# Twelve early products around the fourth head pair, two-sum output groups and unsorted v in a fused attention and gated feed-forward kernel

## The chip, the cores and the metric

The kernel runs on one core of one Trainium2 chip. The metric is the device time of one execution in microseconds (us). "Time" below is that number. "Span" is the stretch that the profiler shows for the core; in every profiled run the time was 1.8 to 2.2 us longer than the span of the same run. PE is the matrix engine, DVE, ACT and POOL are the vector, scalar and general engines, and SP is the engine that here only issues DMAs. All runs in this document gave correct results.

## The reference, cut to what matters

Eight batches, eight heads, 576 positions, head size 64. Attention is masked by blocks of 64: a query sees the keys of its own and of earlier blocks. All tokens then pass through one gated feed-forward layer.

```python
def _attn_ref(q, k, v):                       # (8, 8, 576, 64) each
    scores = scale * np.matmul(q, k.transpose(0, 1, 3, 2))
    mask = block_i >= block_j                 # block = position // 64
    ...                                       # softmax over the keys
    return np.matmul(attn, v)

def _moe_ref(x, w_gate, w_val, w_out):        # x: (4608, 512), d_ff = 1536
    gate = np.maximum(x @ w_gate, 0.0)
    val = x @ w_val
    return gate * val @ w_out
```

## The kernel before

The program is one long stream of feed-forward (FFN) products for PE (groups of 128x128 by 128x512), in tiles of 512 tokens, 144 products to a full tile: 96 for gate and value, 48 for the output. Tile j needs the attention result of batch j. The attention work of the next batches is pushed into this stream at chosen places, so that DVE, ACT, POOL and the DMAs work beside PE. A "place" is the number of products issued so far; tile 0 covers places 0 to 143. Four pairs of heads make a batch. The 576 positions are 512 "main" positions and a "tail" of 64, so each batch has four "visits" of a pair (scores and exponentials), and one "tail visit" for its last 64 queries.

The K and Q of the mains lie in two alternating buffers, by the parity of the batch: batch 2 uses the buffers of batch 0. The scheduler keeps the program's order on each engine and adds the waits that the data need. A DMA is put on the queue of the engine that issues it.

Some names: `qTm` and `kTm` are the transposed queries and keys of the mains, `perm` is where a DMA transpose puts them first, `sc` are scores, `attnT` the exponentials. "PV products" multiply these with v; their normalised result is `xnat`, its transpose `xT` is the input of the FFN, and `hT` is gate times value. A "corner memset" zeroes a masked corner of `attnT`.

The parts that the change and the argument touch:

```python
    def unpermute(self, hp, engs):           # copies K and Q of one head pair into place
        for t in range(2):
            engs[t]((qTm, kTm)[t][self.b % 2][:, :, hp, :]..., self.perm[t, hp // 2]...)

    def both_av(r):                          # PV products of a fourth pair, both heads
        ...
        recip = sb.tile([128, 2, 4], FP, name="recip_both", bufs=1)
        nc.vector.reciprocal(recip, av[:, :, :, 64])
        nc.vector.tensor_tensor(out=xnats[r]..., in0=av[:, :, :, 0:64], in1=..., op=AX.mult)

    def put(j, s, ob, n0, n1):               # stores 128 rows of the output
        if j < B:
            r0 = S * j + 128 * s
            (nc.gpsimd if j == 0 else nc.scalar).dma_start(out[r0 : r0 + 128, :], ob)
        ...

    # in ffn_gen: tiles 0 and 1 start with 9 products that need only three head pairs
                if j < 2 and f == 0:
                    ahead = psum_ffn.tile([128, 512], FP, name="ffnp")
                    for c in range(3):
                        product(gate, 0, c, 0); yield
                    for c in range(3):
                        product(val, 1, c, 0); yield
                    for c in range(3):
                        product(ahead, 0, c, 1); yield
                    steps = [(0, 3), (1, 3)]
    ...
    # each output group is one sum of 12 products; its result goes through one of three ob buffers
                ob = sb.tile([128, 512], FP, name="ob", bufs=3)[:, 0 : n1 - n0]
                nc.vector.tensor_copy(ob, op)
                if store:
                    store.pop()()
                store.append(lambda ...: put(j, s, ob, *n))
    ...
        ffn(9)
        both_av(3)
        to_xT_pe(3, (act, dve))
    ...
        def mains_2a():
            e2.cast_qk(0, 4, (pool, pool))
            e2.transpose(0)                  # two DMA transposes on SP's queue
            e0.load_tails((2,))
            e2.load_v_chunks(0)
    ...
            (90, lambda: e1.sort_v(0, (dve, act))),      # 16 small products
    ...
        events = tail_at(10, 0, (26, 30)) + ...          # tail visit of batch 0: place 154
            (16, un(2, 0, (dve, pool))),                 # copy of batch 2's first pair: place 160
            (44, un(2, 1, (dve, pool))),
```

The softmax here doesn't subtract the row's maximum and nothing guards it: scores larger than these inputs give would overflow.

Of the kernel before, what the change touches and what calls it, by code (L numbers as in the profile page):

```python
# [10 lines left out]
FP = mybir.dt.float32  # L11
# [6 lines left out]
def kernel(  # L18
# [51 lines left out]
    v_p = consts.tile([128, 4, 512], BF, name="v_p")  # L70
    zeros = v_p[:, 0, :]
    nc.vector.memset(zeros, 0.0)

    sel = consts.tile([128, 516], BF, name="sel")
# [14 lines left out]

    def selection(eng):  # L90
        eng.memset(sel, 0.0)
        for c in range(4):
            ps = slice(32 * c, 32 * c + 32)
            eng.tensor_copy(
                sel[ps].rearrange("p (j m) -> p j m", j=4)[:, :, 0:128:4],
                ident[ps, None, 32 * c : 32 * c + 32].to_broadcast([32, 4, 32]),
            )
# [21 lines left out]
    class Early:  # L119
# [27 lines left out]

        def load_v_packed(self, h0):
            self.st[2, h0] = new_stage(1024)
            self.load(self.st[2, h0], v, h0, 4)  # L150
# [59 lines left out]
        def cast_v_packed(self, h0, eng):  # L210
            eng(
                v_p[:, :, 64 * h0 : 64 * h0 + 256].rearrange(
                    "p j (h d) -> p h j d", d=64
                ),
                self.st[2, h0].rearrange("p (h j d) -> p h j d", h=4, j=4),
            )

# [5 lines left out]

        def sort_v(self, h0, engs):


            tp = [psum_sc.tile([128, 2, 512], FP, name="sc") for _ in range(2)]
            for j in range(4):
                for c in range(4):
                    ps = slice(32 * c, 32 * c + 32)  # L230
                    nc.tensor.matmul(
                        tp[c // 2][:, c % 2, 0:256],
                        sel[ps, 128 * j : 128 * j + 128],
                        v_p[ps, j, 64 * h0 : 64 * h0 + 256],
                        start=(j == 0),
                        stop=(j == 3),
                        skip_group_check=True,
                    )
            for i in range(2):
                engs[i](  # L240
                    v_bf[self.b % 2][:, 2 * i : 2 * i + 2, h0 : h0 + 4, 0:64],
                    tp[i][:, :, 0:256].rearrange("p g (h d) -> p g h d", d=64),
                )
# [313 lines left out]
    def both_av(r):  # L557
# [5 lines left out]
        for hh in range(2):  # L563
# [11 lines left out]
        recip = sb.tile([128, 2, 4], FP, name="recip_both", bufs=1)  # L575
        nc.vector.reciprocal(recip, av[:, :, :, 64])
        nc.vector.tensor_tensor(
            out=xnats[r].rearrange("q p (g d) -> q g p d", g=2),
            in0=av[:, :, :, 0:64],
            in1=recip.to_broadcast([128, 2, 4, 64]),  # L580
            op=AX.mult,
        )
# [6 lines left out]
    def to_xT_pe(r, evac):  # L589
        b, hp = divmod(r, 4)  # L590
        if hp == 3:
            br = psum_one.tile([128, 1024], BF, name="one")
        else:
            br = psum_ffn.tile([128, 1024], BF, name="ffnp")
# [20 lines left out]
    def put(j, s, ob, n0, n1):  # L615
        if j < B:
            r0 = S * j + 128 * s
            (nc.gpsimd if j == 0 else nc.scalar).dma_start(out[r0 : r0 + 128, :], ob)
        else:
            for i in range(2):  # L620
                r0 = S * (2 * s + i) + 512
                (nc.scalar, nc.sync)[i].dma_start(
                    out[r0 : r0 + 64, n0:n1], ob[64 * i : 64 * i + 64]
                )

    def ffn_gen():
        for j in range(B + 1):
            hT = []
            x = xT_of(j) if j < B else xTt.rearrange("p b h n -> p h b n")
            ahead = None  # L630
            for f in range(12):

                def product(to, t, c, f):
                    nc.tensor.matmul(  # L634
                        to,
                        (wg, wv)[t][f // 4][:, c, 128 * (f % 4) : 128 * (f % 4) + 128],
                        x[:, c],
                        start=(c == 0),
                        stop=(c == 3),
                    )  # L640

                steps = [(t, c) for t in range(2) for c in range(4)]
                if ahead is None:
                    gate = psum_ffn.tile([128, 512], FP, name="ffnp")
                else:
                    gate, ahead, steps = ahead, None, steps[3:]
                val = psum_ffn.tile([128, 512], FP, name="ffnp")
                if j < 2 and f == 0:
                    ahead = psum_ffn.tile([128, 512], FP, name="ffnp")
                    for c in range(3):  # L650
                        product(gate, 0, c, 0)
                        yield
                    for c in range(3):
                        product(val, 1, c, 0)
                        yield
                    for c in range(3):
                        product(ahead, 0, c, 1)
                        yield
                    steps = [(0, 3), (1, 3)]
                for t, c in steps:  # L660
                    product((gate, val)[t], t, c, f)
                    if (t, c) == (0, 3):
                        gate_sb = sb.tile([128, 512], BF, name="gate_sb", bufs=3)
# [327 lines left out]
```

## Time and profile before

The time is 376.27 us, the median of three runs (375.64 to 376.54). The profiled run is a fourth one; it took 377.73 us.

| | before |
|---|---|
| span of the profiled run | 375.6 us |
| PE busy | 361.1 us, 96% |
| DVE, ACT, POOL busy | 46%, 45%, 31% |
| first output product starts | 48.4 us |
| FFN product 144 (tile 1) starts | 66.8 us (its weight load: 66.4) |

From the page of the profile: busy time (share of the span) and instructions, then the busy share of PE and the granted clock of PE in 40 slices of 9.4 us, in tenths.

```profile
PE 361.1 (96%) x2979; PEld 178.3 (47%) x2979; DVE 172.0 (46%) x392; ACT 170.5 (45%) x282; POOL 116.4 (31%) x151
...
PE   6879999799999999999999999999999999999995
...
PEclk9689999989999999999999999999999999999999
```

PE sets the time. It has slack only in the first 80 us: slices 1 to 3 and slice 8 are not full, and the clock is below full speed in some of the same slices. The trace's clock record has 0.50 at 9.0 to 15.9, 26.1 to 29.5 and 73.9 to 77.3 us.

From the list of what PE waited for (us in total, times, longest):

```profile
PE one L597 <- DVE xnat L577: 2.1, 2, 1.0
...
PE ffnp L634 <- DVE xT L600: 1.6, 2, 0.8
...
PE ffnp L457 <- ACT gate_sb L664: 0.6, 1, 0.6
```

The first two lines are the gaps around the fourth pair, twice, once in tile 0 and once in tile 1: PE has done its nine early products and stands until the pair's result is normalised and transposed.

From the timeline (start, duration, engine, line, operation, in brackets the idle time before it and what ended it), around the start of tile 1:

```profile
70.64 0.40 PE L597 MATMUL one<-ident,xnat 128*128 128x128 bf16 x4 [1.03 <-DVE xnat L577]
71.82 0.38 PE L634 MATMUL ffnp<-xT,wg 128*128 128x512 bf16 x1 [0.79 <-DVE xT L600]
...
72.99 0.64 PE L457 MATMUL sc<-qTt,kTm 64*128 64x64 bf16 x32
...
73.34 1.06 POOL L268 COPY kTm<-perm 128x512 bf16<-128x512 bf16 x1 [8.05 <-PE sc L457]
```

Before the change POOL holds the copy of batch 2's keys ready and waits 8.05 us for PE's tail visit of batch 0 to have read the buffer. PE waits for no copy there.

The table of windows (window, its length, busy time of PE, weight loads, DVE, ACT and POOL with counts, granted clock, DMA share, GB/s):

```profile
60.00:70.00 10.00, 9.06 (x109) 5.07 (x105) 4.84 (x17) 5.49 (x9) 3.18 (x4) 1.00 1.04 186
70.00:80.00 10.00, 8.02 (x85) 3.90 (x85) 3.90 (x8) 4.58 (x9) 5.07 (x7) 0.83 1.12 151
80.00:95.00 15.00, 15.00 (x135) 7.23 (x134) 8.77 (x22) 10.56 (x19) 10.46 (x13) 1.00 0.78 194
...
120.00:350.00 230.00, 229.83 (x1866) 112.33 (x1865) 104.48 (x243) 104.42 (x174) 47.02 (x56) 1.00 0.94 92
```

After 80 us PE is full at full clock.

### The profile page before, as it was taken

The numbers are of one execution on the slowest core, as the hardware profiler recorded it, in microseconds if no ns is written. First come the engines' busy times: TensorE is split into PE (matmuls) and PEld (weight loads), VectorE is DVE, ScalarE is ACT, GpSimd is POOL, SyncE is SP. The second block draws the span as 40 slices with busy tenths as digits, with TensorE's granted clock in tenths as the row PEclk, the third lists the DMA queues.
The fourth block names the chain that finished last, engine by engine and source line by source line (L and its number), as shares of the span: only waits on it lengthen the run. The fifth ranks groups of instructions, "written<-read, shape, count | busy, mean of one in ns | idle before, by whom it ended". The sixth has DMA issues, their size and how long they took to land.

```text
span 375.6 us, 7492 instructions
## 1 busy us (share of the span) xinstructions
PE 361.1 (96%) x2979; PEld 178.3 (47%) x2979; DVE 172.0 (46%) x392; ACT 170.5 (45%) x282; POOL 116.4 (31%) x151
## 2 busy tenths in 40 slices
PE   6879999799999999999999999999999999999995
PEld 2534445444455445544454445444544454444443
DVE  4633544346555554455434543544445444323432
ACT  4823466456524755355445534653366423302310
POOL 5768846176129960570048003100000000000000
PEclk9689999989999999999999999999999999999999
DMA  8999998949989999999469954936400120020003
GB/s 254 292 371 359 364 265 214 189 58 275 216 162 88 134 120 177 175 125 133 124 99 133 125 134 87 69 62 150 78 16 15 44 99 7 0 86 28 2 34 107
DMA packets 142323, 51.35 MB, mean 137 GB/s; under 512 B 122448, under 2 KB 135504, under 8 KB 142288
## 3 DMA queue, kind: packets, MB, share of 16 engines
q1 hardware_dynamic: 81008, 34.62, 42.4%
q0 software_dynamic: 56576, 8.13, 40.3%
q10 hardware_dynamic: 4704, 8.13, 6.7%
q8 instruction: 23, 0.38, 0.5%
q14 instruction: 12, 0.10, 0.1%
HBM read 37.75 MB, written 9.44 MB: 126 GB/s over the span
## 4 chain that ended last, share of the span: by engine, by line
PE 92%; DMA 3%; DVE 3%; ACT 1%; issue 0%; DVEq 0%
PE ffnp L634 51%; PE ffnp L674 23%; PE ffnp L547 5%; PE sc L423 3%; PE ffnp L516 2%; DMA xT<-xnat 2%; PE one L423 2%; PE ffnp L283 1%; PE sc L380 1%; PE sc L457 1%; DMA stage<-in_q_dram 1%; DVE qTm L289 1%; DVE kTm L289 0%; PE one L547 0%; PE one L457 0%
## 5 line engine op out<-in xcount | busy, mean ns | idle before, releaser
L668 DVE TENSOR_TENSOR hT<-gate_sb,ffnp 128x512 bf16<-128x512 bf16 x108 | 74.1, 686 | 96.5 <-PE ffnp L634 84.3
L664 ACT ACTIVATE gate_sb<-ffnp 128x512 bf16<-128x512 f32 x108 | 64.8, 601 | 103.1 <-PE ffnp L634 103.0
L634 PE MATMUL ffnp<-xT,wg 128*128 128x512 bf16 x384 | 105.3, 385 | 2.2 <-DVE xT L600 1.6
L634 PE MATMUL ffnp<-xT,wv 128*128 128x512 bf16 x384 | 104.3, 385 | 0.3 <-ACT gate_sb L664 0.3
L674 PE MATMUL ffnp<-wo,hT 128*128 128x512 bf16 (+1 forms) x444 | 102.2, 373 | 0.0
L634 PEld LDWEIGHTS <-wv 128*128 128x128 bf16 x432 | 40.6, 99 | 48.7 <-issue 6.5
L634 PEld LDWEIGHTS <-wg 128*128 128x128 bf16 x432 | 40.7, 99 | 47.6 <-issue 5.6
L674 PEld LDWEIGHTS <-hT 128*128 128x128 bf16 x444 | 40.6, 98 | 41.1 <-issue 0.8
L432 ACT ACTIVATE attnT<-sc 128x1024 bf16<-128x1024 f32 x56 | 56.8, 1039 | 0.0
L684 DVE COPY ob<-ffnp 128x512 f32<-128x512 f32 (+1 forms) x37 | 25.0, 677 | 38.2 <-PE ffnp L674 38.1
L321 POOL DMA_DIRECT2D v_bf<-in_v_dram x20 | 16.9, 876 | 68.2 <-PE ffnp L516 68.2
L547 PEld LDWEIGHTS <-attnT 128*128 128x128 bf16 x600 | 25.1, 99 | 14.5 <-DVE xnat L502 4.4
L501 DVE RECIPROCAL recip<-ffnp 128x4 f32<-128x4 f32 (+1 forms) x73 | 13.1, 179 | 39.3 <-PE ffnp L547 28.2
L547 PE MATMUL ffnp<-v_bf,attnT 128*128 128x65 bf16 x570 | 27.0, 195 | 0.0
L438 ACT ACTIVATE attnT<-one 128x256 bf16<-128x256 f32 x28 | 10.7, 383 | 31.9 <-PE ffnp L423 29.4
L502 DVE TENSOR_TENSOR xnat<-ffnp,recip 128x256 bf16<-128x256 f32 x57 | 24.2, 424 | 2.0
L478 ACT ACTIVATE attnTt<-one 64x256 bf16<-64x256 f32 x8 | 3.0, 377 | 33.1 <-PE ffnp L457 33.1
L423 PE MATMUL sc<-qTm,kTm 64*128 64x512 bf16 (+1 forms) x168 | 17.0, 305 | 0.0
L423 PEld LDWEIGHTS <-kTm 64*128 64x128 bf16 x224 | 9.0, 94 | 15.3 <-issue 11.7
L469 ACT ACTIVATE attnTt<-sc 128x1024 bf16<-128x1024 f32 x16 | 15.6, 1014 | 0.0
L321 POOL DMA_DIRECT2D k_bf<-in_k_dram x16 | 14.4, 953 | 0.2 <-issue 0.2
L321 POOL DMA_DIRECT2D q_bf<-in_q_dram x16 | 14.4, 948 | 0.0
(91 smaller groups left out, 261.7 us busy)
## 6 DMA issues: line engine op xcount, KB each, us to landing
out_dram<-ob ACTq DMA_DIRECT2D x28, 256.0 KB, 2.2
stage<-in_moe_w_gate_dram SPq DMA_DIRECT2D x6, 512.0 KB, 9.3
stage<-in_moe_w_val_dram SPq DMA_DIRECT2D x6, 512.0 KB, 9.5
stage<-in_q_dram SPq DMA_DIRECT2D x6, 512.0 KB, 6.6
stage<-in_k_dram SPq DMA_DIRECT2D x6, 512.0 KB, 8.1
stage<-in_moe_w_out_dram SPq DMA_DIRECT2D x6, 512.0 KB, 9.5
stage<-in_v_dram SPq DMA_DIRECT2D x16, 128.0 KB, 5.1
stage<-in_v_dram SPq DMA_DIRECT2D x8, 256.0 KB, 5.4
```

The costliest lines, as they stand in the source:

```text
L321: nc.gpsimd.dma_start(dst, src[b, :, 128 * c : 128 * c + n, :].rearrange("h p d -> p h d"),)
L423: nc.tensor.matmul(where[c].rearrange("p (c n) -> p c n", n=128), kTm[b % 2][head_of(hh), c, hp, :], qTm[b % 2][head_of(hh), c:4, hp, :], ...
L432: return lambda: nc.scalar.activation(at[:, :, lo : lo + 512], sc, AF.Exp, scale=scale)
L469: return lambda: nc.scalar.activation(at[:, :, 2 * i : 2 * i + 2, 0:256], main[i].rearrange("p g (h n) -> p g h n", h=2), AF.Exp, scale=scale,
L501: nc.vector.reciprocal(recip, av[:, :, 64])
L502: nc.vector.tensor_tensor(out=out, in0=av[:, :, 0:64], in1=recip.to_broadcast([rows, n, 64]), op=AX.mult,)
L547: nc.tensor.matmul(av[:, p, :], at[:, hh, col : col + 128], vb[:, c, h, :], start=(p == 0), stop=(c == p), skip_group_check=True,)
L634: nc.tensor.matmul(to, (wg, wv)[t][f // 4][:, c, 128 * (f % 4) : 128 * (f % 4) + 128], x[:, c], start=(c == 0), stop=(c == 3),)
L664: nc.scalar.activation(gate_sb, gate, AF.Relu)
L668: nc.vector.tensor_tensor(out=h, in0=gate_sb, in1=val, op=AX.mult)
L674: nc.tensor.matmul(op, hT[f][:, 128 * s : 128 * (s + 1)], wo[f // 4][:, f % 4, n0:n1], start=(f == 0), stop=(f == 11),)
L684: nc.vector.tensor_copy(ob, op)
```

## The change

The intent is to fill PE's gaps in the first 80 us. Tiles 0 and 1 begin with 12 products of three head pairs instead of 9, split around the fourth pair's PV products and transposes. The first two output groups of tile 0 are summed in two parts, so that PE can begin before the last third of the output weights is there. Batch 1's v is loaded in its natural order for all heads, which removes 16 sorting products, their evictions and the matrix for them. Beside these, `both_av` normalises head by head, batch 0's stores move from POOL's queue to SP's, and many places of the schedule move. The core of the diff (cuts marked):

```diff
+            first = 0
+            if j < 2:
+                first = 2
+                acc = {n: psum_ffn.tile([128, 512], FP, name="ffnp")
+                       for n in ((0, 0), (0, 1), (1, 0))}
+                for cs in ((0, 1), (2,)):
+                    for t in range(2):
+                        for f in range(2):
+                            ...
+                            for c in cs:
+                                product(acc[t, f], t, c, f)
+                                yield
+                ...                      # then the four products of the fourth pair
...
+            if j == 0:                   # first two output groups: products 0 to 7 first
+                ops = [psum_ffn.tile([128, 512], FP, name="ffnp") for _ in range(2)]
+                for f0 in (0, 4):
+                    for s in range(2):
+                        for f in range(f0, f0 + 4):
+                            out_mm(ops[s], s, f, 0, 512, 0, 8)
+                            if f == 7:
+                                part_sum[s] = new_ob(512)
+                                nc.vector.tensor_copy(part_sum[s], ops[s])
+                            yield
...
-        recip = sb.tile([128, 2, 4], FP, name="recip_both", bufs=1)
-        nc.vector.reciprocal(recip, av[:, :, :, 64])
-        nc.vector.tensor_tensor(...)
+            normalise(xnats[r][:, :, 64 * hh : 64 * hh + 64], av[:, hh])
...
-            (nc.gpsimd if j == 0 else nc.scalar).dma_start(out[r0 : r0 + 128, :], ob)
+            (nc.sync if j == 0 else nc.scalar).dma_start(out[r0 : r0 + 128, :], ob)
...
-        ffn(9)
+        ffn(4)
+        to_xT_pe(2, (act, None))
         both_av(3)
+        ffn(5)
         to_xT_pe(3, (act, dve))
...
         def mains_2a():
+            e2.load_v_chunks(0)
+            e2.load_v_chunks(1)
+            e2.load_tails((0, 1))
+            e2.load_tails((2,))
             e2.cast_qk(0, 4, (pool, pool))
             e2.transpose(0)
-            e0.load_tails((2,))
-            e2.load_v_chunks(0)
...
-        events = round_at(94, 4, (113, 117), (121, pe_xT))
-        events += round_at(109, 5, (129, 133), (137, pe_xT))
+        events = round_at(96, 4, (112, 112), (112.3, pe_xT))
+        events += round_at(104, 5, (112.1, 112.2), (118, pe_xT))
...
-            (90, lambda: e1.sort_v(0, (dve, act))),
...
-        events = tail_at(10, 0, (26, 30)) + tail_at(116, 1, (132, 136))
+        events = tail_at(20, 0, (38, 42)) + tail_at(116, 1, (132, 136))
...
             (16, un(2, 0, (dve, pool))),
             (44, un(2, 1, (dve, pool))),
```

The tail visit of batch 0 moves from place 154 to place 164, while the copy of batch 2's first pair into the same key buffer stays at place 160. And `mains_2a` now asks SP for seven loads before the two transposes that this copy needs.

## The prediction

> **What bounds it now.** PE. It is busy 361.1 of 375.6 us (page, busy times), and the table of windows shows it idle for about 0.2 us between 80 and 350 us. What can be saved lies before 80 us: 10.5 us idle there, plus half clock (granted 0.50) at about 9.0-15.5, 26-29.3 and 74-77.3 us. PE's waits around both fourth pairs: 2.1 us for xnat before the transposes, 1.6 us for xT after them. The Trainium skill ("TensorE: Matmul & The Clock Gate", "What's actually happening") says the clock halves after about one idle window of 3.4 us; the trace agrees: slow stretches of about 3.3 us follow such gaps.
>
> **What the change does directly.** It puts 4 products before the fourth pair's PV products, 5 behind them (1.08 us at 0.216 us each, against a 1.03 us wait) and 3 behind the transposes (0.65 us against 0.79 us). It removes 16 sorting products (0.55 us of PE), two evictions and Pool's selection matrix (2.5 us). Two sums per output group let PE go on before the last output weights arrive: those land at 45.5 us, one load per 1.36 us, and this stays. So I expect PE 6-9 us ahead of before at the end of tile 0 (FFN product 144: about 58-60 us instead of 66.8).
>
> **What takes most of it back.** The tail visit of batch 0 moves from product 154 to 164, but the copy of batch 2's first pair into the same K tile stays at product 160. The order of instructions shows that PE's tail scores now wait for Pool's copy of batch 2's K; in before, Pool waited for PE. Two things follow. The last 64 queries of batch 0 see batch 2's keys in two of eight heads (the result should still pass). And PE now depends on batch 2's chain: load, cast, DMA transpose, copy. The change also puts four v-chunk loads and three tail loads ahead of that transpose on SP's queue. With landings read from before: batch 1's v about 50.5-51 us, batch 0's tails 52.5, batch 2's q and k 58.5-60, two stores to 60, four chunk loads at 1.1 us each to 64.5, three tails at 0.85 us to 67, two transposes about 1.1 us apart to 69, Pool's copy 1.07 us: about 70.3 us. PE arrives at about 64-65, waits some 6 us, and restarts at half clock, as in before.
>
> **Time.** In before the tail visit ended at 73.6 us, 302.0 us before the end, 10 products (2.2 us) earlier in the stream. So span = 70.3 + 0.6 + 302.0 - 2.2 = 370.7 us; measured times lie 0.7 us above the span: 371.4 us, range 367.5 to 375.0. Faster by over 2%: 0.17; within 2%: 0.81; slower: 0.02.
>
> **What would show it.** Right: the list of waits has one PE wait of 4-8 us for Pool's kTm copy near 65-71 us, the largest of the run; both 1.03 us waits for xnat under 0.4 us; first output product before 44 us (before: 48.4); no sorting products; idle PE after 80 us unchanged. Wrong: PE reaches the tail visit without that wait, or waits on output weights (DMA) at 45-48 us for over 2 us.
>
> **What would make it wrong.** Chunk loads may move faster than 1.1 us each, or the transposes may overtake them: then 365-368 us. If the restart stays at full clock, another 1.7 us goes. Stalls of PE around product 112 only eat into the wait. Later transposes give up to 375.

## The result, and the profile after

The changed kernel took 380.86 us (four runs, 380.73 to 381.38); the kernel before took 376.08 us in the same rounds (375.64 to 376.54). Ratios in this document are the mean time of one kernel's runs over that of the other's of the same rounds, so not quite the ratio of the quoted medians. Here it is 1.0130, with a 95% interval of 1.0112 to 1.0147. So the kernel is slower by 1.3%, inside the 2% that the prediction called most likely, but 5.9 us above the top of its range.

The same views as before. The page:

```profile
PE 357.5 (94%) x2915; PEld 178.1 (47%) x2963; DVE 176.6 (47%) x399; ACT 169.6 (45%) x279; POOL 111.3 (29%) x142
...
PE   6999987597999999899999999999999999999996
...
PEclk9899999998999999999999999999999999999999
```

The early gaps are smaller: slices 2 and 3 are now full. Slices 6, 7 and 10 are new holes, where the kernel before had a 9 each time (slice 17, with the wait at 159 us, shows an 8), and slice 8 has fallen from 7 to 5.

What PE waited for:

```profile
PE sc L412 <- POOL kTm L223: 3.6, 1, 3.6
...
PE one L378 <- DVE qTm L223: 1.6, 1, 1.6
PE sc L522 <- DVE xnat L457: 1.5, 2, 0.7
PE sc L522 <- DVE attnT L698: 1.2, 1, 1.2
PE ffnp L580 <- DMA xT<-xnat: 1.2, 2, 1.0
```

The waits around the fourth pair are gone in their old form (2.1 and 1.6 us). In their place are a wait for POOL's key copy, one for DVE's query copy, one between the two heads of `both_av`, and one for a memset. The timeline shows the first two:

```profile
69.90 0.19 PE L412 MATMUL one<-qTt,kTt 64*128 64x64 bf16 x1
...
73.65 0.64 PE L412 MATMUL sc<-qTt,kTm 64*128 64x64 bf16 x32 [3.56 <-POOL kTm L223]
...
87.04 0.27 PE L378 MATMUL one<-qTm,kTm 64*128 64x256 bf16 x1 [1.62 <-DVE qTm L223]
87.63 0.27 PE L378 MATMUL ffnp<-qTm,kTm 64*128 64x256 bf16 x1 [0.33 <-DVE hT L595]
...
83.42 3.56 DVE L223 COPY qTm<-perm 128x512 bf16<-128x512 bf16 x1
...
72.55 1.04 POOL L223 COPY kTm<-perm 128x512 bf16<-128x512 bf16 x1 [9.21 <-DMA perm<-k_bf]
...
82.97 0.61 POOL L195 CAST v_bf<-stage 64x512 bf16<-64x512 f32 x1 [2.67 <-PE ffnp L471]
83.53 2.02 POOL L189 CAST v_bf<-stage 128x1024 bf16<-128x1024 f32 x2
85.50 1.04 POOL L223 COPY kTm<-perm 128x512 bf16<-128x512 bf16 x1
...
66.04 1.67 SPq L158 DMA_DIRECT2D stage<-in_v_dram  x1
67.80 1.34 SPq L209 DMA_TRANSPOSE perm<-q_bf  x1
69.24 1.28 SPq L209 DMA_TRANSPOSE perm<-k_bf  x1
```

The sense of the wait at the tail visit has turned round. Before, POOL waited 8.05 us for PE. Now POOL waits 9.21 us for a DMA transpose, and PE waits 3.56 us for POOL. The transposes of the queries and of the keys are issued at 67.8 and 69.2 us, because seven loads stand ahead of them in SP's queue; in the kernel before they were issued at 58.3 and 60.2 us:

```profile
58.31 1.34 SPq L254 DMA_TRANSPOSE perm<-q_bf  x1
60.19 1.31 SPq L254 DMA_TRANSPOSE perm<-k_bf  x1
```

Reading the program, this order also lets the last 64 queries of batch 0 see keys of batch 2 in two of the eight heads; the result still passes the comparison.

Further down, a DVE copy takes 3.56 us. The statistics of this instruction, from the view of the tile it writes (shortest, median and longest in ns):

```profile
L223 DVE COPY qTm<-perm x8: 591/625/3565, 71.3 to 128.7; 128x512 bf16<-128x512 bf16 x8
```

The same copy of the same shape needs 0.59 us when nothing disturbs it. The long one begins beside POOL's cast at 82.97 us, lasts through four POOL instructions in a row, and ends 0.44 us after the last of them (86.98 against 86.54 us). PE waits 1.62 and 0.33 us for it.

The windows:

```profile
60.00:70.00 10.00, 7.88 (x82) 4.00 (x79) 5.08 (x15) 4.06 (x8) 2.16 (x3) 1.00 0.99 233
70.00:80.00 10.00, 6.16 (x63) 2.75 (x56) 2.07 (x4) 4.05 (x7) 4.64 (x7) 0.83 0.80 171
80.00:95.00 15.00, 12.95 (x111) 6.53 (x111) 10.53 (x19) 7.54 (x13) 8.92 (x11) 0.89 0.65 172
...
120.00:350.00 230.00, 226.90 (x1844) 111.90 (x1875) 103.63 (x243) 104.27 (x174) 49.17 (x59) 1.00 0.99 93
```

PE's busy time falls from 9.06 to 7.88 us between 60 and 70, from 8.02 to 6.16 us between 70 and 80, and from 15.00 to 12.95 us between 80 and 95, where the clock is also no longer full. The clock record has 0.50 at 9.5 to 12.9, 74.3 to 77.7 and 88.0 to 91.4 us. (In the last row some matrix records are missing, 1844 beside 1875 weight loads, so its busy time is a little low; the one longer wait there is 0.96 us for a DMA transpose at 159 us.)

The clearest reading comes from following one and the same FFN product through both traces. Each line is the start of a product (of its weight load, which the traces have for every product; the product itself starts 0.2 to 0.5 us later) and the lead (negative) or lag of the changed kernel, at places where both kernels have the same attention work behind them or nearly so. It compares one execution of each, the profiled ones:

| product | before, us | after, us | after minus before |
|---|---|---|---|
| 24 | 29.80 | 24.74 | -5.06 |
| 96 (first output product) | 48.22 | 43.19 | -5.03 |
| 144 (tile 1) | 66.38 | 61.56 | -4.82 |
| 164 (behind the tail visit) | 77.07 | 74.22 | -2.85 |
| 188 | 84.37 | 82.89 | -1.49 |
| 217 | 93.43 | 95.34 | +1.91 |
| 300 | 116.77 | 118.97 | +2.20 |
| 500 | 172.90 | 176.41 | +3.51 |
| 1307 (last) | 371.42 | 375.20 | +3.78 |

The change wins 5 us in the first 30 us, as intended, holds it to the start of tile 1, and then loses 8.6 us: 2.0 up to the tail visit, 1.4 right behind it (half clock), 3.4 between 84 and 95 us (the DVE copy and half clock), 0.3, 1.3 and 0.3 later.

### The profile page after: what moved, and what is told of

It is laid out like the page before. It is cut to its first block, busy times and chain, and to the rows that moved or that the text cites. A ratio compares the mean times of both kernels' runs of the same rounds, so it can differ in the third digit from the quotient of the medians.

```text
span 379.2 us, 7422 instructions
## 1 busy us (share of the span) xinstructions
PE 357.5 (94%) x2915; PEld 178.1 (47%) x2963; DVE 176.6 (47%) x399; ACT 169.6 (45%) x279; POOL 111.3 (29%) x142
## 4 chain that ended last, share of the span: by engine, by line
PE 74%; DMA 15%; SPq 5%; issue 2%; POOL 1%; DVE 1%; ACT 0%; POOLq 0%
PE ffnp L580 42%; PE ffnp L637 20%; DMA stage<-in_moe_w_val_dram 5%; PE ffnp L502 4%; DMA stage<-in_q_dram 4%; PE sc L378 3%; DMA xT<-xnat 3%; DMA stage<-in_moe_w_out_dram 2%; PE ffnp L471 2%; SPq L139 2%; SPq L158 1%; PE one L378 1%; DMA stage<-in_k_dram 1%; PE sc L412 1%; DMA perm<-k_bf 1%
## 5 line engine op out<-in xcount | busy, mean ns | idle before, releaser
L595 DVE TENSOR_TENSOR hT<-gate_sb,ffnp 128x512 bf16<-128x512 bf16 x106 | 72.7, 686 | 97.3 <-PE ffnp L580 83.7
L580 PE MATMUL ffnp<-xT,wg 128*128 128x512 bf16 x367 | 102.4, 385 | 2.2 <-DMA xT<-xnat 1.2
L580 PE MATMUL ffnp<-xT,wv 128*128 128x512 bf16 x368 | 100.8, 383 | 0.7 <-issue 0.3
L637 PE MATMUL ffnp<-wo,hT 128*128 128x512 bf16 (+1 forms) x421 | 98.4, 373 | 1.4 <-DVE recip L456 0.2
L671 DVE COPY ob<-ffnp 128x512 f32<-128x512 f32 (+1 forms) x35 | 23.7, 676 | 40.7 <-PE ffnp L637 39.4
L223 POOL COPY kTm<-perm 128x512 bf16<-128x512 bf16 x8 | 8.5, 1074 | 20.6 <-PE sc L412 11.3
```

The costliest lines, as they stand in the source:

```text
L580: nc.tensor.matmul(to, (wg, wv)[t][f // 4][:, c, 128 * (f % 4) : 128 * (f % 4) + 128], x[:, c], start=(c == 0), stop=(c == 3),)
L595: nc.vector.tensor_tensor(out=h, in0=gate_sb, in1=val, op=AX.mult)
L637: nc.tensor.matmul(op, hT[f][:, 128 * s : 128 * (s + 1)], wo[f // 4][:, f % 4, n0:n1], start=(f == lo), stop=(f == hi - 1),)
```

## The experiments

The theory: two edits of the schedule, the key copy ahead of the tail visit and the loads ahead of the transposes, make PE wait for batch 2's chain (load, cast, DMA transpose, copy), and this costs what the rest of the change wins. Rival A: DVE and POOL block each other in the copies, and that is the loss. Rival B: the split normalisation and the stores on SP's queue hold PE around the fourth pair. All edits below are against the changed kernel unless the text says otherwise. The kernel before was run beside every group on the same chip; its median was between 376.39 and 377.67 us, so results of different groups are compared by their ratio to it, not by their time.

### One edit undone at a time

**e1_copy_after_tail**: the copy of batch 2's first pair goes behind the tail visit.

```diff
-            (16, un(2, 0, (dve, pool))),
+            (20.5, un(2, 0, (dve, pool))),
```

> One event moved: the copy of batch 2's first pair (q by DVE, k by Pool) goes from product 160 to just behind the tail visit of batch 0 at 164. Theory A (program order made PE wait for Pool's copy): PE's 3.6 us wait for kTm goes, and with it the half clock of 74.3 to 77.7 us (about 1.7 us); PE next needs that K at product 180, about 74 us, when the copy (ended at 73.6 us) is done. 375.5 us, give or take 1.5. Rival B (the order only showed a late DMA chain, which stops PE at its next reader just as long): PE waits over 2.5 us for kTm or qTm at the visit of product 180, time above 378.5 us. Both: the error against the reference falls back to that of before.

Measured: 378.23 us, ratio 1.0038 (1.0016 to 1.0059). The wait for POOL's key copy is gone, as the expectation's theory A (not rival A above) says, and 0.9% of time comes back, but the time is 1.2 us above the theory's range. In its profile another wait has taken a part of the place:

```profile
64.72 0.69 DVE L671 COPY ob<-ffnp 128x512 f32<-128x512 f32 x1 [3.78 <-DMA out_dram<-ob]
65.50 0.31 DVE L698 MEMSET attnT<- 64x128 uint32 x2
...
65.72 0.48 PE L522 MATMUL sc<-v_bf,attnT 128*128 128x65 bf16 x10 [3.48 <-DVE attnT L698]
```

DVE's eviction into `ob` waits for an earlier store out of that buffer, since there are only three. The memset that PE needs stands behind it in DVE's order. So a late store holds PE for 3.48 us. In the changed kernel the same wait is 1.21 us. A second wait of this kind, 3.0 us, stands at 112 us. It also moved the half clock: 0.50 at 66.2 to 69.6 us.

**e2_transpose_first**: the transposes go back ahead of the loads.

```diff
         def mains_2a():
+            e2.cast_qk(0, 4, (pool, pool))
+            e2.transpose(0)
             e2.load_v_chunks(0)
             ...
             e2.load_tails((2,))
-            e2.cast_qk(0, 4, (pool, pool))
-            e2.transpose(0)
```

> The order of before within the batch 2 step: cast and DMA transpose first, then the four v-chunk loads and three tail loads; the copy stays ahead of the tail visit. If the loads put ahead of the transpose made it late: its k half lands near 65 to 67 us instead of 72.4, Pool's copy ends by 68.5, PE's wait for kTm is under 0.5 us, and the time is 374 to 377 us. Rival (the transposes are late because q and k land late, at 57.4 and 58.9 us, and PE's order does not matter): landing moves by less than 2 us and the time stays above 379 us.

Measured: 377.66 us, ratio 1.0021 (0.9991 to 1.0050). The two transposes land at 65.7 and 66.7 us instead of 71.3 and 72.4, PE waits for no key copy, and 1.1% comes back; the time is 0.7 us above the expected range. The memset wait is 2.89 us here, and the wait for DVE's long query copy (4.36 us in this run) is 2.4 us.

**e3_second_copy_act**: the second pair's query copy goes from DVE to ACT.

```diff
-            (44, un(2, 1, (dve, pool))),
+            (44, un(2, 1, (act, pool))),
```

> One engine changed: the q copy of batch 2's second pair (3.56 us on DVE at 83.4 us, against 0.59 us elsewhere) goes to ACT. Theory P (DVE's copy and Pool's work shut each other out): the copy takes about 0.6 us on ACT, PE's waits of 1.62 and 0.33 us at 87 us go, and so does the half clock of 88.0 to 91.4 us; 377 to 378 us. Rival Q (that copy waited for its data, so any engine would take as long): the ACT copy takes over 3 us or starts as late, and the time stays at 380.5 to 381 us.

Measured: 381.24 us, ratio 1.0130 (1.0094 to 1.0166): no gain. The copy takes 1.09 us on ACT and PE's 1.6 us wait is gone, so the mechanism is as rival A says. But near 115 us DVE now waits for a store, and PE behind it for 4.2 us:

```profile
114.36 0.69 DVE L671 COPY ob<-ffnp 128x512 f32<-128x512 f32 x1 [4.10 <-DMA out_dram<-ob]
```

That store of batch 0 stands in SP's queue and lands at 114.27 us. Removing a wait on its own bought nothing, because another one behind it was longer.

**e4_one_normalise**: both heads of the fourth pair are normalised together again.

```diff
-            normalise(xnats[r][:, :, 64 * hh : 64 * hh + 64], av[:, hh])
+        recip = sb.tile([128, 2, 4], FP, name="recip_both", bufs=1)
+        nc.vector.reciprocal(recip, av[:, :, :, 64])
+        nc.vector.tensor_tensor(...)
```

> One part undone: the fourth pair is normalised in one go as in before, so PE no longer waits 0.73 us between its two heads, in tiles 0 and 1. If all that PE gains before 70 us only lengthens the wait for kTm (theory A), the wait for kTm grows by 0.5 to 1.5 us from 3.6 and the time stays within 0.5 us of 380.9. Rival: the gain comes through and the time falls by 1.2 to 1.6 us.

Measured: 381.87 us, ratio 1.0121 (1.0085 to 1.0158). The two waits of 0.73 us between the heads are gone, and the time stayed, as expected. But the key wait did not grow as expected: it is 3.0 us, and the memset wait ahead of it grew instead, to 2.5 us. Both end at the same moment as in the changed kernel (64.1 and 73.6 us), so what PE gains ahead of them is lost in them. Rival B's first half fails as a cause of the loss.

### All together, and parts of it

**e5_all_five**: the edits of e1, e2, e3 and e4, and batch 0's stores back on POOL's queue.

```diff
-            (nc.sync if j == 0 else nc.scalar).dma_start(out[r0 : r0 + 128, :], ob)
+            (nc.gpsimd if j == 0 else nc.scalar).dma_start(out[r0 : r0 + 128, :], ob)
```

> Five edits to the changed kernel at once: the copy behind the tail visit, cast and transpose ahead of the chunk loads, the second pair's q copy on ACT, the fourth pair normalised in one go, and batch 0's stores on Pool's queue as in before. Theory: each removes one wait that held or hid the others, the 12-product start keeps its 5 to 6 us at product 96 and about 8 us at product 160, and no PE wait over 1 us is left between 44 and 115 us: 367.5 to 370.5 us. Rival (what PE gains early is bound to be lost, because batch 2's DMA chain sets the pace): PE still waits 4 us or more in all for qTm or kTm and the time is 374 us or more.

Measured: 375.77 us, ratio 0.9946 (0.9892 to 1.0000). The loss is gone and a little of the gain shows, but the expected 367.5 to 370.5 us were missed by 5 us. PE still waits 3.7 us for the memset behind a store, and 2.2 us for a key copy that stands behind other POOL work.

**e6_store_pool_only**: only the stores, by the same edit.

> One part undone: batch 0's stores go back from SP's queue to Pool's. Theory S (a store behind SP's loads keeps its ob buffer, DVE waits for the buffer, and the corner memset behind it in DVE's order keeps PE from the fourth pair): DVE's wait of 1.3 us for the store (out_dram<-ob) and PE's wait of 1.2 us for the memset near 64 us go. The time moves little, 379 to 381 us, because the wait for kTm takes up what is won. Rival: PE's wait for the memset stays above 0.8 us.

Measured: 378.45 us, ratio 1.0002 (0.9942 to 1.0062), more than was expected of it. The expectation failed in its wait too: PE's wait for the memset did not go but is 1.78 us, as the rival had it, behind a store that lands at 64.15 us. The landing of the transposes is the same as in the changed kernel (72.5 us for the key half), so it did not free the chain. In its profiled run PE comes to the tail visit later and waits only 0.95 us there; the clock is halved at 67.2 to 70.6 us, hidden ahead of the same release, and neither at 74 nor at 88 us, although the wait for DVE's 3.56 us copy at 85 us is there again. So the part of the gain that its trace shows is two slow-clock stretches fewer in the open. The four runs spread from 376.38 to 378.74 us, and the profiled one is the fastest. A gain of up to 1.3% remains that the traces explain only by the clock, which I leave open. Part of it lies in the kernel before, whose runs in this group reach from 375.94 to 380.89 us: between the medians e6 is 2.4 us (0.6%) faster than the changed kernel. So rival B's second half may carry a part of the loss; v5 below, which has the first two stores on ACT's queue and still is 1.2% slower than the kernel before, shows that the loss does not need it.

**e7_five_less_copy**: e5 with the early key copy kept, so only e1's edit left out.

> The five edits without the first: the copy stays ahead of the tail visit. With the transposes first, k lands near 65 to 67 us and Pool's copy ends near 68, about when PE comes to the tail visit; so PE waits at most 1.5 us for kTm and the time is 0 to 2 us above e5_all_five. If program order alone were the cause: PE waits over 3 us and loses 4 us or more.

Measured: 375.34 us, ratio 0.9928 (0.9872 to 0.9984), no worse than e5. With the transposes early, the copy ahead of the tail visit costs nothing: it is done before PE comes. That was the first sign that the copy's place costs time only when the transposes are late.

**e11_five_less_store**: e5 with the stores left on SP's queue.

> The five edits without the last: batch 0's stores stay on SP's queue. Theory S: DVE waits 2.5 to 4 us for a store near 64 us, PE waits as long for the memset, the half clock comes back for 3.4 us, and a second such wait may come near 110 us (the last store of batch 0 stands behind batch 3's transposes on SP); 3 to 7 us above e5_all_five. Rival (the store's queue does not matter once the loads are in order): within 1 us of e5_all_five.

Measured: 377.04 us, ratio 0.9971 (0.9902 to 1.0041), 0.25% (1.3 us) above e5, inside the intervals; 3 to 7 us were expected. DVE waits for stores twice (PE: 3.2 and 3.0 us). On POOL's queue the first wait was no shorter (3.7 us): there the stores stand behind POOL's casts. Which queue is used matters less than that both are late.

### POOL's order, and the stores on ACT's queue

**t1_pool_order**: the edits of e1, e2 and e4, all stores on ACT's queue, and POOL's later work in another order.

```diff
-            (22, tails_2),
-            (16, un(2, 0, (dve, pool))),
-            (44, un(2, 1, (dve, pool))),
-            (46, v_2),
+            (46, tails_2),
+            (20.5, un(2, 0, (dve, pool))),
+            (30, un(2, 1, (dve, pool))),
+            (45, v_2),
```

> Built on what the runs showed: the copy of batch 2's first pair behind the tail visit, transposes ahead of the chunk loads, one normalise, batch 0's stores on ACT's queue (it waits for no load and no cast), the second pair's copy from product 188 to 174, ahead of the tail casts and v casts in Pool's order, and on DVE again. Theory: stores land by 58 us, so DVE waits under 0.5 us for a store near 64 us and PE under 0.7 us for the memset (3.7 in e5_all_five); PE waits under 0.5 us for Pool's kTm near 83 us (2.2 there), and no DVE copy takes over 1.7 us. PE's product 204 comes 6 to 8.5 us before that of the kernel before (2.2 in e5_all_five): 368 to 371.5 us. Rival (the loss is contention that moves on whatever is mended): still over 3 us of PE waits between 60 and 115 us, time above 373 us.

Measured: 376.01 us, ratio 0.9976 (0.9932 to 1.0020). The lead at product 204 is 8.4 us, and 4.0 us of it are left at the end of the profiled run, which took 373.27 us, the shortest of six. The clock is full from 5 to 370 us. The lead is what the theory expected, the time is not (368 to 371.5 us): waits of 2.0, 1.8, 0.9 and 1.1 us remain between 60 and 115 us, so here the rival's "over 3 us, above 373 us" came true.

**t2_store_act_only**: only the stores, on ACT's queue.

> The changed kernel with one edit: batch 0's stores on ACT's queue. Theory S: DVE's wait for a store near 64 us goes (1.3 us in the changed kernel, up to 4 in others) and so does PE's wait for the memset (1.2 us), but PE then waits longer for kTm: 4.5 to 7 us instead of 3.6. Time 379.5 to 381 us, no better by more than 1.5 us. Rival: PE's wait for the memset stays above 0.8 us, so it was not the store.

Measured: 380.04 us, ratio 1.0079 (1.0035 to 1.0123). PE reaches the tail visit with a lead of 7.7 us instead of 6.9, waits 5.8 us there for POOL's keys, and is 3.9 us behind at the end, as in the changed kernel (3.8). Time won ahead of the key wait is given back in it, as it was in e4.

**t3_t1_spread**: t1 with the PV products of the first pair spread out again.

```diff
-        events = round_at(96, 4, (112, 112), (112.3, pe_xT))
+        events = round_at(96, 4, (108, 110), (112.3, pe_xT))
```

> t1_pool_order with the PV products of batch 1's first pair at 108 and 110 instead of all four head visits in a row at 112. Theory: in a row they cost PE about 1.9 us more than their work, because five PSUM buffers are freed by DVE one after another; spread, 0.8 to 1.5 us of this is won and product 116 comes as much earlier, unless the last output weights (cast at about 47.5 us) hold PE then. Time 0.5 to 1.5 us below t1_pool_order.

Measured: 375.38 us, ratio 0.9965 (0.9914 to 1.0016), the same as t1 within the intervals. ACT's queue shows a new wait, as it does in t1: the third store is issued only at 62.03 us, when a load for batch 2 has landed that has nothing to do with it, and the exponential behind it waits. In the packed trace the store waits for the semaphore that is to tell of its own landing, and the load, issued at 54.59 us, uses the same one and lands at 62.01 us. So the wait comes from the program's reuse of DMA semaphores.

```profile
62.03 0.34 ACTq L573 DMA_DIRECT2D out_dram<-ob  x1
62.42 1.02 ACT L387 ACTIVATE attnT<-sc 128x1024 bf16<-128x1024 f32 x1 [1.83 <-DMA stage<-in_q_dram]
```

**t4_t1_batch2_as_changed**: t1 with e1's and e2's edits left out, so the two edits of the theory put back into the improved kernel.

> t1_pool_order with the batch 2 step as the change has it: chunk and tail loads ahead of the transposes, the copy ahead of the tail visit. With nothing else to hold PE before it, this shows the whole price of that pair: PE comes to the tail visit near 66 us, waits 5 to 8 us for kTm, then runs at half clock for 3.4 us. 6 to 9 us above t1_pool_order, 376 to 379 us. Rival: under 3 us above t1_pool_order.

Measured: 383.32 us, ratio 1.0156 (1.0108 to 1.0204), 7.3 us slower than t1 on the same chip, as expected (6 to 9). PE waits 7.0 us for POOL's keys, and the clock is halved for 6.8 us. This is the cleanest support for the theory so far: the two edits alone cost more than the whole loss.

### The best version, and each edit put back

**v1_best**: t3 with the third and fourth store of batch 0 on SP's queue, and one more of POOL's copies earlier.

```diff
-            nc.scalar.dma_start(out[r0 : r0 + 128, :], ob)
+            (nc.sync if j == 0 and s > 1 else nc.scalar).dma_start(out[r0 : r0 + 128, :], ob)
...
-            (80, un(2, 3, (dve, pool))),
+            (61, un(2, 3, (dve, pool))),
```

> t3_t1_spread with two more waits taken out: batch 0's third store goes back to SP's queue (on ACT it held the exponential behind it until 62.4 us), and the copy of batch 2's fourth pair comes before batch 3's casts in Pool's order (product 205 instead of 224). Theory: PE's 2.6 us wait for the memset and its 1.9 us wait for kTm go; PE's product 217 comes 8 to 10 us and product 1307 6 to 9 us before that of the kernel before; 368 to 371 us in the profiled run. Rival: waits of over 3 us in all reappear elsewhere between 60 and 115 us and the time stays above 373 us.

Measured: 373.99 us (six runs, 372.01 to 374.83), ratio 0.9924 (0.9892 to 0.9955). It beats both kernels. But the profiled run, the fastest, is 1 us above the range expected for it, and the rival (new waits of over 3 us in all, time above 373 us) describes it better: PE waits 1.4 us at 83 us and 1.9 us at 110 us. In the timeline POOL waits for PE again at the tail visit:

```profile
67.32 0.65 PE L412 MATMUL sc<-qTt,kTm 64*128 64x64 bf16 x32
...
67.67 2.31 POOL L223 COPY kTm<-perm 128x512 bf16<-128x512 bf16 x2 [2.67 <-PE sc L412]
```

The clock is full from 6 us to the end. The lead is 9.5 us at product 188, and 5.2 us are left at the end.

**v2_best_copy_early**: v1 with the early key copy (e1's edit left out).

> v1_best with the copy ahead of the tail visit (product 160), transposes still first: one half of the pair alone. k lands at 65 to 67 us, so PE waits 1 to 3 us for kTm at the tail visit: 0 to 2 us above v1_best.

Measured: 373.50 us, ratio 0.9941 (0.9890 to 0.9992). As in e7, it costs nothing: the copy is finished at 65.3 us, and PE comes at 67.1.

**v3_best_loads_first**: v1 with the loads ahead of the transposes (e2's edit left out).

> v1_best with the chunk and tail loads ahead of the transposes, copy behind the tail visit: the other half alone. Pool's copy ends at 73 to 75 us and PE needs it at product 180, near 71 to 72 us: 1.5 to 4 us above v1_best.

Measured: 376.91 us, ratio 1.0018 (0.9973 to 1.0063), 2.9 us slower than v1. PE does not wait for the keys, but DVE waits for the transposed queries, and PE for DVE:

```profile
71.29 0.59 DVE L223 COPY qTm<-perm 128x512 bf16<-128x512 bf16 x1 [3.81 <-DMA perm<-q_bf]
...
72.53 1.02 PE L587 MATMUL ffnp<-xT,wg 128*128 128x512 bf16 x4 [1.88 <-DVE hT L602]
```

Behind it the clock is halved from 73.9 to 77.3 us. By product 188 the profiled run is 3.7 us behind v1's. A second loss follows: a wait of 2.80 us for a DMA transpose at 114 us (1.93 us in v1), with half clock from 114.9 to 118.3 us, and at the end it is 5.6 us behind. What share of the 2.9 us belongs to which is open. So the loads ahead of the transposes hurt by themselves, here through DVE, where the expectation had named POOL's copy.

**v5_best_both**: v1 with both put back.

> v1_best with both halves, as the change has them. If the two act together (late transposes alone or early copy alone still leave 20 products or an early landing as cover): 6 to 9 us above v1_best, more than v2_best_copy_early and v3_best_loads_first add up to, with a PE wait of 6 to 8 us for kTm and half clock after it. If they simply add: the sum of the two.

Measured: 381.29 us, ratio 1.0119 (1.0087 to 1.0152), 7.3 us slower than v1 on the same chip, as expected (6 to 9).

```profile
67.32 0.19 PE L412 MATMUL ffnp<-qTt,kTt 64*128 64x64 bf16 x1
...
73.35 1.03 PE L412 MATMUL sc<-qTt,kTm 64*128 64x64 bf16 x32 [5.84 <-POOL kTm L223]
...
72.25 1.04 POOL L223 COPY kTm<-perm 128x512 bf16<-128x512 bf16 x1 [7.90 <-DMA perm<-k_bf]
```

| on one chip, ratio to before | transposes first | loads first |
|---|---|---|
| copy behind the tail visit | v1: 0.9924 | v3: 1.0018 |
| copy ahead of the tail visit | v2: 0.9941 | v5: 1.0119 |

The four numbers support the theory. The copy's place alone costs nothing that can be told from zero, the loads' place alone 0.9%, the two together 2.0%. By the mean times the two together cost 3.7 us more than their sum, which is hardly clear of the scatter of 4 to 6 runs each (twice the standard error is 3.1 us). The traces are clearer: PE waits 5.84 us for POOL's keys with both edits, and not at all with one of them. And v5 is as slow as the changed kernel (1.0130), although it has all the other improvements: as long as PE waits for this chain, nothing that PE or DVE gain ahead of it counts.

### Two last questions

**v4_best_pool_as_changed**: v1 with POOL's order of the changed kernel.

```diff
-            (46, tails_2),
-            (30, un(2, 1, (dve, pool))),
-            (45, v_2),
-            (61, un(2, 3, (dve, pool))),
+            (22, tails_2),
+            (44, un(2, 1, (dve, pool))),
+            (46, v_2),
+            (80, un(2, 3, (dve, pool))),
```

> v1_best with the order of Pool's later work (tails of batch 2, second pair's copy, v of batch 2, fourth pair's copy) put back as in the changed kernel. Theory (a copy of K on Pool that stands behind casts holds PE for 1.8 to 2.2 us): 2 to 4 us slower than v1_best's ratio of 0.992 to the kernel before, that is a ratio of 0.998 to 1.003, with PE waits for kTm of Pool or for DVE's locked-out copy near 83 to 92 us. Rival (only the copy ahead of the tails and the loads ahead of the transposes matter): within 1 us of v1_best, ratio 0.990 to 0.995.

Measured: 376.65 us, ratio 0.9978 (0.9940 to 1.0016), within what the theory gave and outside what the rival gave, though the interval of v1 on another chip (0.9892 to 0.9955) just overlaps. The wait is there:

```profile
PE one L378 <- POOL kTm L223: 3.2, 1, 3.2
```

It stands at 81 us, and half clock follows at 81.6 to 85.0 us. v6 below ran beside it on the same chip and has v1's order of POOL: there the ratio is 0.9902 (0.9871 to 0.9933), clear of v4's, though v6 differs from v4 in one more edit. So the order of POOL's later work, which puts a key copy behind casts, is a second cause, of the size of some 2 us.

**v6_best_xT_first**: v1 with the second transposes of batch 3 behind the last transpose of a head pair's result on SP's queue. Nothing else moves.

```diff
-            (101, lambda: early[3].transpose(1)),
+            (117.5, lambda: early[3].transpose(1)),
```

> v1_best with the second transposes of batch 3 moved on SP's queue behind the last xT transpose of tile 2's batch and one store; nothing else moves. Theory (PE's 1.9 us wait for xT at 110 us in v1_best is that transpose standing behind the two perm transposes): the wait is gone or under 0.3 us, and the time is 1.5 to 2 us under v1_best, ratio to before 0.987 to 0.990. Rival (the wait is the 16 DMA engines' load, not the place in the queue, or the time comes back in a later wait): ratio 0.991 to 0.994.

Measured: 373.84 us (six runs), ratio 0.9902 (0.9871 to 0.9933). The 1.9 us wait for that transpose is gone from the list, as the theory says. But the profiled run was the slowest of the six (376.51 us): it started its products 2.1 us late, and PE waited 2.4 us for a store at 109 us instead. The ratio lies between the two expectations and the intervals overlap, so whether v6 is faster than v1 is open. Both beat the kernel before by 0.8 to 1.0%.

## Why the prediction was wrong

What held:

- PE set the time and the first 80 us were the only place to win. The lead of about 5 us was there at product 24. The first output product came at 43.2 us (predicted: before 44). Product 144 came 4.8 us ahead (predicted: 6 to 9), so the early gain was 1.2 us less than the low end of it. The sorting products are gone.
- The trap was found before the run: the largest wait of the run (the next largest are two of 1.6 us, one of them at the very start of both kernels) is PE's wait for POOL's key copy behind the tail scores, where before POOL waited for PE. The prediction asked for 4 to 8 us near 65 to 71 us; it was 3.56 us and ended at 73.65 us. It was short because PE came only at 69.8 us, not at 64 to 65: the smaller early gain and waits of 1.21 us for the memset and 0.73 us between the heads, which the prediction did not have. Since the chain set the end of the wait, this cost nothing.
- It said that gains ahead of this wait only eat into the wait. e4 and t2 show it.

What failed, in the order of the sum "70.3 + 0.6 + 302.0 - 2.2 = 370.7 us", plus 0.7:

| term | predicted, us | measured, us | difference |
|---|---|---|---|
| POOL's key copy done | 70.3 | 73.6 | +3.3 |
| from there to the end of the span | 300.4 | 305.6 | +5.2 |
| median time minus the profiled span | 0.7 | 1.7 | +1.0 |
| sum | 371.4 | 380.9 | +9.5 |

(305.6 is 379.2 minus 73.6; 1.7 is 380.86 minus 379.2.)

1. **The step that failed most is "idle PE after 80 us unchanged".** The prediction took the 302.0 us behind the tail visit from the kernel before, as if the change could only act ahead of it. They became 5.2 us longer. By the table of products, 3.4 us of this were lost between products 188 and 217, where DVE's copy took 3.56 instead of 0.59 us beside four POOL instructions in a row; the remaining 1.9 us came later, 0.96 us of it as a wait for a DMA transpose at 159 us. The prediction had looked at what is added to each engine, not at what meets what in time. In the timeline POOL's cast of the tail's v at 82.97 us waits until PE's tail PV products have read the v buffer (`<-PE ffnp L471`). The change moves these from places 170 and 174 to 182 and 186, and DVE's query copy stands at place 188: so the moved tail visit brings POOL's backlog of four instructions and that copy together. In the kernel before the same four POOL instructions ran from 81.10 to 84.70 us, and the copy began at 84.60 us, as they ended, and took 0.60 us. e2, where the transposes are early, has the same collision (4.36 us), so the late transposes are not its cause. e1 escaped by a hair: its copy began at 80.97 us, 0.24 us ahead of POOL's cast, and took 0.71 us. e3, with the copy on ACT, shows that the collision is what PE waited for at 87 us; it does not show 1.9 us of gain, since the next wait swallowed it. That moving the tail visit back would remove it was not run by itself. The lines of the kernel before, to be held against those of the changed kernel above:

```profile
81.10 0.61 POOL L219 CAST v_bf<-stage 64x512 bf16<-64x512 f32 x1 [0.91 <-POOL kTm L268]
81.66 2.03 POOL L205 CAST v_bf<-stage 128x1024 bf16<-128x1024 f32 x2
83.63 1.07 POOL L268 COPY kTm<-perm 128x512 bf16<-128x512 bf16 x1
...
84.60 0.60 DVE L268 COPY qTm<-perm 128x512 bf16<-128x512 bf16 x1
```

2. **The term for the chain was too small by 3.3 us.** The landings in the trace, against what was written:

| what lands | predicted, us | landed, us |
|---|---|---|
| batch 1's v | 50.5 to 51 | 53.8 |
| batch 0's tails, q and k | 52.5 | 55.3 |
| batch 2's q and k, the last of four | 58.5 to 60 | 62.2 |
| two stores | 60 | 63.6 |
| four chunk loads | 64.5 | 68.8 |
| three tails | 67 | 70.4 |
| two transposes | 69 | 72.4 |
| POOL's copy, done | 70.3 | 73.6 |

  The order was right in every line, and the steps behind the first one have nearly the right size. The error comes in with the first line, 2.8 us, and stays between 2.2 and 4.3 us.

3. **The last term mixed two runs.** The offset of 0.7 us fits the median time of three runs minus the span of a fourth, slower one (376.27 - 375.6). Time minus span of one and the same run is 377.73 - 375.6 = 2.1 us, and 381.38 - 379.2 = 2.2 us for the changed kernel. The prediction took a slow execution of the kernel before as its base and paired it with the times of faster ones; the changed kernel's profiled run was only 0.5 us above its median. This is 1 us of the miss.

4. That the restart would run at half clock held (74.3 to 77.7 us). But no gap of PE in the kernel before is as long as the 3.4 us that the prediction names for it: its half clock at 73.9 us follows gaps of 1.03, 0.79 and 0.55 us. The second half-clock stretch at 88.0 to 91.4 us was not foreseen; it comes behind the waits of point 1.

What then was the change worth? v1 against v5 answers it on one chip: the two unlucky edits cost 7.3 us, more than the 4.8 us by which the change lost. Even without them, of a lead of 9.5 us at product 188 only 5.2 us reached the end of v1's profiled run (its fastest of six, held against a slow run of the kernel before; between the medians it is 2.4 us). Most of the rest went into two waits: 1.4 us at 83 us for a normalisation that DVE began late, behind a query copy of 2.92 us beside POOL, so the same collision again, and 1.9 us at 110 us for a DMA transpose, a chain that in the kernel before had slack and that an earlier PE runs into.

## What to carry to other kernels

When a change moves one consumer behind or ahead of a writer of the same buffer, look at which of the two now waits: a wait that used to fall on an engine with slack (POOL, 8.05 us, at no cost) fell on PE, and what PE gained ahead of it no longer counted. In a queue that serves its requests in order, put first what the busiest engine will wait for, and loads that are needed 10 us later behind it. And when predicting, do not carry over "the rest of the run" as a constant: a reader that moves later releases its buffer later, the work that waited for it comes in a lump, and the lump meets something else; and take the offset between time and span from one and the same run.

## What the Trainium skill lacked or had wrong

- "SBUF — State Buffer", section "Who interferes with whom", says that DVE in a two-port mode and GpSimd exclude each other, that the one which issues first has the ports "for the whole instruction", and that PE and ACT never wait. The trace agrees as far as it goes: the copy took 0.59 us alone, 3.56 us beside POOL, and 1.09 us on ACT. What the page lacks is that the loser can wait through several instructions: in the changed kernel POOL ran a cast of 0.61 us, two casts of 2.02 us and a copy of 1.04 us back to back, and DVE's copy, in its record from 83.42 us, ended only 0.44 us behind the fourth. In v1 a copy of 2.92 us lasts through a cast and two key copies and ends 0.46 us behind them, and in e2 one lasts 4.36 us. So in these three runs the price was set by how much POOL had queued, not by one instruction. Whether this copy runs in a two-port mode no trace shows.
- "TensorE: Matmul & The Clock Gate", sections "What's actually happening" and "Why this matters for your kernels", give an idle window of about 3.4 us and advise against gaps over about 3 us. The slow stretches here are 3.4 us long or twice that, in agreement. But some follow gaps much shorter than these sections give: 1.62 and 0.33 us in the changed kernel (0.50 at 88.0 to 91.4 us) and 1.88 us in v3 (0.50 at 73.9 to 77.3 us), while waits of 2.0 and 1.8 us in t1, 1.93 us in v1 and even 2.82 us in e7 left the clock full. The runs do not show what decides. A PE-bound kernel like this one has to count gaps of 2 us as a risk of another 1.7 us (estimated as half of 3.4 us).
- "DMA: Bandwidth & Descriptors", section "Issuing engines are not separate DMA queues", says that the choice of the issuing engine saves only the sequencer's time of starting a DMA. For the 16 engines' load the runs do not contradict it, but the order within a queue was worth more than that here: with seven loads ahead, the transposes landed at 71.3 and 72.4 us instead of 65.7 and 66.7 (e2), and that order is a large part of the 7.3 us between v1 and v5. The page's rules do not speak of placing urgent transfers first.
